# Early row maxima of a second attention layer: a fourth unit of queries, groups dealt out evenly, values ahead of the last score

## The chip, the cores and the metric

The kernel runs on one core of one Trainium2 chip. The metric is device time in microseconds (us) of one execution of the whole program, lower is better. Three runs of the kernel before the change took 2326.10, 2326.68 and 2327.10 us; the median is 2326.68 us. Engines are called by the profile's names: PE is the matmul engine (PEld is its weight load), DVE the vector engine, ACT the scalar engine, POOL the GpSimd engine, SP the queue that issues most DMAs.

## The reference

Two identical layers, with the same weights, on x of 2048 rows by 448: attention with 16 query heads of 28 that share one key head and one value head, then a gated linear unit.

```python
def _A_ref(x, wq, wk, wv, wo):              # H = 16, Dh = 28, S = 2048, D = 448
    q = (x @ wq).reshape(B, S, H, Dh).transpose(0, 2, 1, 3)
    k, v = x @ wk, x @ wv
    scores = jnp.einsum("bhqd,bkd->bhqk", q, k) * (Dh ** -0.5)
    o = jnp.einsum("bhqk,bkd->bhqd", softmax(scores), v)
    return o.transpose(0, 2, 1, 3).reshape(B, S, H * Dh) @ wo
def _B_ref(x, w_gate, w_up, w_down):        # F = 1792
    return (sigmoid(x @ w_gate) * (x @ w_up)) @ w_down

for _ in range(2):
    x = x + _A_ref(_layernorm(x), wq, wk, wv, wo)
    x = x + _B_ref(_layernorm(x), w_gate, w_up, w_down)
```

## The kernel before

**Tiles and steps.** A layer has 16 units of 128 queries (`u`) and 16 tiles of 128 keys (`kt`). The attention of a layer is a loop of 256 steps, one for each pair (u, kt), unit after unit. A step makes four score tiles of 128 keys by 512 (four heads by 128 queries) in PSUM (`s`, L591), ACT takes the exponential of each into a tile `P` (L594), and PE multiplies the four `P` of the step before with the values into one accumulator (`pv`, L602). The scores go into the exponential with the row maximum taken off already: the maximum of a query is one more row of the stationary operand `QS`.

**Row maxima.** So the maxima of a unit must be there before its first score. `Maxima` finds them with a pass of its own: the 2048 keys fall into ranges and the 16 heads into four sets, which gives 16 groups for each unit (for unit 0 of the second layer the last 512 keys are cut finer). A group is four matmuls side by side into four PSUM tiles `mx` (L556) and four DVE reductions `mp` (L561). After a unit's last group `row_max` closes it: two DVE operations, and a step later (`late`, `LT`) a transpose `mt` on PE, a copy `mr` on DVE and a DMA issued by POOL that puts the maxima into `QS` (L585). Groups of the first layer run one a step (`M` in `ORDER`), some unit ahead of the scores.

**PSUM.** One accumulator bank belongs to `pv`. All other PSUM tiles (`s`, `mx`, `qp`, `dn`, `wo`, `mt` and so on) share seven banks. A group of maxima takes four of them at once, and the next scores take what comes free.

**Other work of PE.** Between the pieces of a step, `fill.slice` (the `F` of `ORDER`) puts in matmuls of the rest of the layer: query projections `qp`, the gated unit (`gp`, `up`, `dn`) of blocks of 256 rows, and the output projection `wo` of a finished unit. A planner spreads what there is over the steps (`rate`). In the first 49 steps of the second layer there is little: eight query projections. The first block of the gated unit can start only when two units of attention are done and have passed through `Block.tile`, a list of stages that `tick` runs, each a given number of steps after the one before. Stage `fd` is the normalisation `xn` (L340) of such a unit on DVE; it reads a row factor `rs`, which six small POOL operations (L317 to L322) make.

**The seam between the layers.** The first layer ends with a loop that is no step of attention (L1088): it finishes the last gated blocks (`dn`, 42 matmuls for each 128 rows), and each 128 rows that are done give the next layer's keys: sum `x` (L801), statistics and `xn` on DVE, split `hl`, transposes `t`, key projection `kv`, `ktl`, transposes `kvt`. The second layer's first score needs the maxima of unit 0 over all keys, so it waits for the very last rows. While it waits, the loop takes early groups of the second layer: those of units 0, 1 and 2 (`AHEAD`) whose keys end at 1536 or before (`soon`), one in every two turns. The loop ends when all of them are done (`started`). What is left of units 1 and 2, and the first groups of later units, is done in the second layer's first 48 steps: in every even step, and in steps 5 and 11.

**Order.** Every engine works its instructions in the order in which the Python code issues them. The two lines that set it here:

```python
ORDER = "FSFSFSFSPXM"                                      # L1016
n = step % 2 == 0 or step in (5, 11)                       # L1051, second layer
```

Of the kernel before, what the change touches and what calls it, by code (L numbers as in the profile page):

```python
# [8 lines left out]
F32 = mybir.dt.float32  # L9
F16 = mybir.dt.float16  # L10
# [9 lines left out]
def interleaved_layers_kernel(ctx: ExitStack, tc: tile.TileContext, x, wq, wk, wv, wo, wg, wu, wd, out, layers=2):  # L20
# [6 lines left out]
    nc = tc.nc  # L27
# [3 lines left out]
    NT, NB, G, KT, FC = S // 128, S // 512, H // 4, S // 128, F // 128  # L31
    U = NT
# [429 lines left out]
    def load_qh(l, u):  # L462
        b, t = divmod(u, 4)
        if l + b == 0:
            QH[l, u] = QH0[:, :, t * 128:(t + 1) * 128]
            return
        assert QDONE[l, b] == G
        q = wk1.tile([128, G, 128], F16, name="QH", bufs=3)
        QH[l, u] = q
        nc.sync.dma_start(q, qd[l % 2][b, :, 0, :, t * 128:(t + 1) * 128].rearrange("g p n -> p g n"))  # L470

# [15 lines left out]
            out += [(kb, ka, kz, list(range(g, g + n))) for g in range(0, G, n)]  # L487
        return out

    AHEAD = (1, 2)  # L490

    def soon(u, kz):

        return (u == 0 or u in AHEAD) and kz <= S - 512

    class Maxima:
# [28 lines left out]

        def started(self):

            return not any(a[0] == 0 or soon(a[0], self.need(a)) for a in self.todo)

        def visit(self):  # L530
            for i in range(len(late) - 1, -1, -1):
# [4 lines left out]
        def step(self, a=None):  # L536
# [8 lines left out]
            todo = groups_of(l, u)  # L545
            kb, ka, kz, gs = todo[j]
            if u not in self.mp:
                self.mp[u] = wk1.tile([128, 4, 4, NB + 2], F32, name="mp", bufs=4)
            mp, qh = self.mp[u], QH[l, u]
            assert KVD[l] * 128 >= kz  # L550
            n, w = len(gs), kz - ka
# [20 lines left out]
    def row_max(l, u, mp, n):  # L572

        m32 = wk1.tile([128, 16], F32, name="m32")
        m16 = wk1.tile([128, 16], F16, name="m16")
        nc.vector.tensor_reduce(m32, mp.rearrange("p g h k -> p (g h) k")[:, :, :n], axis=AX.X, op=OP.max)
        nc.vector.tensor_scalar(m16, m32, -(2.0 ** -15), None, op0=OP.mult)

        def fin():
            stored.add(("m", l, u))  # L580
            p = fps([16, 128], F16, "mt")
            nc.tensor.transpose(p, m16, id16)
            r = wk1.tile([16, 128], F16, name="mr")
            nc.vector.tensor_copy(r, p)
            nc.gpsimd.dma_start(QS[l, u][28:29].rearrange("o g h n -> o (g h) n"), r)  # L585
        late.append([LT, fin, (l, u)])

    def scores(l, u, kt, g, P):
        assert ("m", l, u) in stored, (l, u, kt)
# [39 lines left out]
    class Block:  # L629
# [8 lines left out]
        def tile(self, u):  # L638
# [90 lines left out]
                return  # L729
                yield  # L730
            slow = 2 if l == 0 and u < 4 else 1
            return (1, f0), (1, fx), (slow, fy), (1, fz), (1, fw), (slow, fa), (slow, fb), (2, fc), (3, fd), (3, fe), (2, ff)

        def load_w(self, f):
            need(2 + f)
# [279 lines left out]
    early[0] = False  # L1015
    ORDER = "FSFSFSFSPXM"  # L1016
    MORE = (5, 10)
    HEAD = (U * KT - 32, U * KT - 28, U * KT - 16)
    FIRST = KT * TB + 17
    KEEP = 28000  # L1020
    VS = 1800
    for l in range(layers):
# [3 lines left out]
            late.pop(0)[1]()  # L1026
        if not l:
            mx.step()
        if not final:
            layer_tiles(l + 1)  # L1030
        if l:
# [5 lines left out]
        rate = 0.0  # L1037
        for step in range(U * KT):
            u, kt = divmod(step, KT)
            if step in HEAD and not final:  # L1040
                if step == HEAD[0]:
                    mxs[l + 1] = Maxima(l + 1)
                else:
                    load_qh(l + 1, HEAD.index(step))
            P = []
            for o in ORDER:
                if o == "S":
                    scores(l, u, kt, len(P), P)
                elif o == "M":
                    if l and step < KT * (1 + len(AHEAD)):  # L1050
                        n = step % 2 == 0 or step in (5, 11)  # L1051
                    else:
                        n = 1 + (u == 0 and kt in MORE)
                    if not n:
# [33 lines left out]
        while side or pend or (fill.gens if final else not nx.started()):  # L1088
# [5 lines left out]
            if a:  # L1094
                kz = nx.need(a)
                if soon(a[0], kz):
                    go = n >= 2
                elif kz == S - 128:
                    go = len(fine) > 1
                else:  # L1100
                    go = True
                if go:
                    nx.step(a)
                    n = 0
# [25 lines left out]
```

## Time and profile before

| quantity | value |
|---|---|
| median of three runs | 2326.68 us |
| the profiled execution, whole | 2324.3 us |
| its span, first to last instruction | 2321.3 us |
| mean granted clock of PE over the span | 0.987 |
| PE busy | 2225.1 us, 96% |
| DVE busy | 1638.1 us, 71% |
| ACT busy | 1585.8 us, 68% |
| POOL busy | 339.4 us, 15% |
| first score of the second layer | 1249.71 us from the span's start |
| first 48 steps of the second layer | 1250.1 to 1394.4 us |

How to read it: a busy share of 96% is an average over parts that differ. PE's spans are modelled and overlap the ones behind them, so a short wait of PE shows as a gap only where it is longer than that overlap; the distance from the start of one matmul to the start of the next shows it better. The idle time in square brackets of a timeline row is the engine's idle time just before that row, with the instruction that ended it.

### The profile page before, as it was taken

To read this page: it belongs to the slowest core of one execution; us is meant where nothing else is said; L and a number is where in the kernel's file an instruction comes from. 1 tells how busy PE (TensorE), PEld (TensorE's weight loads), DVE (VectorE), ACT (ScalarE), POOL (GpSimd) and SP (SyncE) were. 2 spreads that over 40 slices of the span, in tenths; PEclk is the share of its full clock that TensorE was granted. 3 is DMA by queue.
4 is the path that set the end of the run, shared out by engine and by line. 5 is a ranking of instruction groups with operands and counts; after the bars stand their busy time and mean duration, and the time that the engine had idled before them with its cause. 6 is when DMAs were issued, how large, how long until landed. Compare 5 with 4: busy or idle time off the path is not lost.

```text
span 2321.3 us, 41368 instructions
## 1 busy us (share of the span) xinstructions
PE 2225.1 (96%) x15786; PEld 1004.9 (43%) x15786; DVE 1638.1 (71%) x2908; ACT 1585.8 (68%) x2614; POOL 339.4 (15%) x606
## 2 busy tenths in 40 slices
PE   5898899999999999999999999999999999999999
PEld 3222244444444444444563224444444444444456
DVE  6888887777777777777884557767677777767322
ACT  6698777677767777776515887767676767767731
POOL 6204762100110110101002010000000000000010
PEclk9799999999999999999999999999999999999999
DMA  4244671423313132332341113223231313223233
GB/s 118 68 118 126 203 223 41 107 76 95 101 61 108 44 110 73 95 98 76 106 132 40 30 54 100 78 83 98 72 87 57 107 47 105 68 83 95 76 101 114
DMA packets 205639, 213.28 MB, mean 92 GB/s; under 512 B 137520, under 2 KB 165872, under 8 KB 205440
## 3 DMA queue, kind: packets, MB, share of 16 engines
q1 hardware_dynamic: 200064, 195.77, 28.9%
q0 software_dynamic: 5376, 14.87, 1.9%
q8 instruction: 123, 2.02, 0.4%
q14 instruction: 76, 0.62, 0.1%
HBM read 175.37 MB, written 23.59 MB: 86 GB/s over the span
## 4 chain that ended last, share of the span: by engine, by line
PE 57%; DVE 3%; DMA 1%; ACT 1%; issue 1%; SPq 0%; POOL 0%; DVEq 0%; POOLq 0%; ACTq 0%
PE pv L602 13%; PE s L591 12%; PE dn L791 8%; PE up L363 8%; PE gp L363 8%; PE mx L556 4%; DVE mp L561 2%; PE wo L702 2%; PE qp L363 1%; ACT P L594 1%; DMA wgu<-wgu_d 1%; SPq L459 0%; DVE oT L683 0%; DVE th L761 0%; DMA XT<-hl 0%
## 5 line engine op out<-in xcount | busy, mean ns | idle before, releaser
L594 ACT ACTIVATE P<-s,esc 128x512 f32<-128x512 f32 x2048 | 1323.8, 689 | 460.4 <-PE s L591 434.0
L561 DVE TENSOR_REDUCE mp<-mx 128x1 f32<-128x512 f32 x2048 | 1269.8, 683 | 422.0 <-PE mx L556 419.7
L591 PE MATMUL s<-QS,KK 96*128 96x512 f16 x2048 | 767.6, 383 | 42.4 <-DVE mp L561 20.8
L363 PEld LDWEIGHTS <-wgu 128*128 128x128 f16 x4928 | 457.9, 97 | 239.0 <-issue 95.9
L602 PE MATMUL pv<-P,VV 128*32 128x512 f32 x4096 | 548.8, 608 | 0.0
L363 PE MATMUL gp<-XT,wgu 128*128 128x256 f16 x2464 | 375.0, 273 | 0.0
L363 PE MATMUL up<-XT,wgu 128*128 128x256 f16 x2464 | 373.9, 273 | 0.5 <-ACT P L594 0.4
L791 PE MATMUL dn<-WD,h 128*128 128x448 f16 x1344 | 321.0, 353 | 0.0
L591 PEld LDWEIGHTS <-KK 96*128 96x128 f16 x2048 | 197.5, 97 | 155.6 <-issue 60.4
L556 PE MATMUL mx<-KK,QH 32*128 32x512 f16 (+1 forms) x2080 | 222.3, 386 | 10.0 <-ACT P L594 4.0
L556 PEld LDWEIGHTS <-QH 32*128 32x128 f16 x2080 | 53.9, 91 | 393.1 <-issue 390.6
L791 PEld LDWEIGHTS <-h 128*128 128x128 f16 x1344 | 124.1, 98 | 137.7 <-issue 25.5
L602 PEld LDWEIGHTS pv<-P,VV 128*32 128x32 f32 x4096 | 81.1, 108 | 200.4 <-issue 198.0
L764 ACT ACTIVATE h<-th 128x512 f16<-128x512 f32 x112 | 70.3, 628 | 108.5 <-DVE th L761 108.3
L676 POOL TENSOR_TENSOR lb<-pvs,lb 128x512 f32<-128x512 f32 x32 | 40.9, 1278 | 608.3 <-DMA lb<-sums 517.1
L317 POOL TENSOR_SCALAR rs<-mv 128x1 f32<-128x1 f32 (+2 forms) x52 | 12.2, 234 | 797.1 <-DVE mv L302 757.1
L363 PE MATMUL qp<-XT,WQ 128*128 128x512 f16 x352 | 117.7, 400 | 1.9 <-DVE mp L561 0.7
L765 DVE SCALAR_TENSOR_TENSOR h<-th,h 128x512 f16<-128x512 f32 x112 | 78.9, 704 | 34.5 <-ACT h L764 34.5
L753 ACT ACTIVATE th<-gp,gsc 128x512 f32<-128x512 f32 x112 | 76.6, 684 | 38.5 <-PE gp L363 38.4
L761 DVE SCALAR_TENSOR_TENSOR th<-th,up 128x512 f32<-128x512 f32 x112 | 76.1, 680 | 37.3 <-PE up L363 30.9
L702 PE MATMUL wo<-WO,oT 128*128 128x448 f16 x384 | 94.7, 358 | 4.4 <-ACT oT L682 4.3
L363 PEld LDWEIGHTS <-WQ 128*128 128x128 f16 x352 | 34.1, 100 | 67.2 <-issue 43.5
(134 smaller groups left out, 847.2 us busy)
## 6 DMA issues: line engine op xcount, KB each, us to landing
wgu<-wgu_d SPq DMA_DIRECT2D x224, 512.0 KB
QS<-qd SPq DMA_DIRECT2D x384, 32.0 KB
lb<-sums SPq DMA_DIRECT2D x128, 64.0 KB
xr<-in_A_x_dram SPq DMA_DIRECT2D x32, 224.0 KB
qd<-qst POOLq DMA_DIRECT2D x28, 256.0 KB, 2.6
wgu_d<-sgu POOLq DMA_DIRECT2D x14, 512.0 KB, 3.8
QH<-qd SPq DMA_DIRECT2D x28, 128.0 KB
x2d<-x SPq DMA_DIRECT2D x16, 224.0 KB
```

Source lines behind the costliest of these rows:

```text
L363: nc.tensor.matmul(ps, a, b, start=n == 0, stop=n == 10)
L556: nc.tensor.matmul(ps[h][:, i * w:(i + 1) * w], qh[32 * h:32 * h + 32, g], KK[l][32 * h:32 * h + 32, 1, ka:kz], start=True, stop=True, til ...
L561: nc.vector.tensor_reduce(o, ps[h].rearrange("p (g k) -> p g k", g=n), axis=AX.X, op=OP.max)
L591: nc.tensor.matmul(s, KK[l][0:96, 0, kt * 128:(kt + 1) * 128], QS[l, u][:, g].rearrange("p h n -> p (h n)"), start=True, stop=True)
L594: nc.scalar.activation(p, s, AF.Exp, scale=esc)
L602: nc.tensor.matmul(v[32 * g:32 * g + 32], VV[l][:, kt], P[g], start=kt == 0, stop=kt == KT - 1, tile_position=(0, 32 * g))
L702: nc.tensor.matmul(p, v["oT"][:, a, h * 128:(h + 1) * 128], WO[:, c, h], start=n == 0, stop=n == 11)
L753: defer(lambda: nc.scalar.activation(th, gp.rearrange("p j n -> p (j n)"), AF.Tanh, scale=gsc))
L761: nc.vector.scalar_tensor_tensor(t, th, 1.0, up.rearrange("p j n -> p (j n)"), op0=OP.add, op1=OP.mult)
L764: nc.scalar.activation(h[:, 0], t, AF.Copy, scale=2.0 ** -17)
L765: defer(lambda: nc.vector.scalar_tensor_tensor(h[:, 1], t, 2.0 ** -17, h[:, 0], op0=OP.mult, op1=OP.subtract), 1)
L791: nc.tensor.matmul(p, hs[f // 2][:, a, o:o + 128], WD[:, f, c], start=n == 0, stop=n == 3 * FC - 1)
```

## The change

Five edits, all for the second layer's first units:

- `AHEAD` takes in unit 3, and `started` asks only for unit 0's groups: the seam no longer has to finish the early groups. In the seam they are taken as long as `fine` is empty, that is, until the last 128 rows' `dn` is done.
- What is left of units 0 to 3, and two groups more, is dealt out evenly over the first 47 steps (`sparse`); here 21 groups where 26 stood in 48 steps.
- In a step behind one with a group, `LATER` sets the order: the values of the step before stand ahead of the fourth score, not behind it.
- The stage `fd` of the second layer's units 0, 1 and 2 comes one step later (4 steps behind the stage ahead of it, not 3).
- The maxima of units 1 to 3 are closed two visits after their last reduction, not one. The high halves of the first 512 queries are loaded at once into one tile `QHB` and the pool `QH` has two buffers, not three; `mp` has five, not four.

```diff
@@ -465,7 +465,14 @@
             QH[l, u] = QH0[:, :, t * 128:(t + 1) * 128]
             return
         assert QDONE[l, b] == G
-        q = wk1.tile([128, G, 128], F16, name="QH", bufs=3)
+        if b == 0:
+            if t == 0:
+                q = big.tile([128, G, 512], F16, tag="big", name="QHB")
+                nc.sync.dma_start(q, qd[l % 2][b, :, 0].rearrange("g p n -> p g n"))
+                for i in range(4):
+                    QH[l, i] = q[:, :, i * 128:(i + 1) * 128]
+            return
+        q = wk1.tile([128, G, 128], F16, name="QH", bufs=2)
         QH[l, u] = q
         nc.sync.dma_start(q, qd[l % 2][b, :, 0, :, t * 128:(t + 1) * 128].rearrange("g p n -> p g n"))
 
@@ -487,7 +494,7 @@
             out += [(kb, ka, kz, list(range(g, g + n))) for g in range(0, G, n)]
         return out
 
-    AHEAD = (1, 2)
+    AHEAD = (1, 2, 3)
 
     def soon(u, kz):
 
@@ -525,7 +532,7 @@
 
         def started(self):
 
-            return not any(a[0] == 0 or soon(a[0], self.need(a)) for a in self.todo)
+            return not any(a[0] == 0 for a in self.todo)
 
         def visit(self):
             for i in range(len(late) - 1, -1, -1):
@@ -545,7 +552,7 @@
             todo = groups_of(l, u)
             kb, ka, kz, gs = todo[j]
             if u not in self.mp:
-                self.mp[u] = wk1.tile([128, 4, 4, NB + 2], F32, name="mp", bufs=4)
+                self.mp[u] = wk1.tile([128, 4, 4, NB + 2], F32, name="mp", bufs=5)
             mp, qh = self.mp[u], QH[l, u]
             assert KVD[l] * 128 >= kz
             n, w = len(gs), kz - ka
@@ -583,7 +590,7 @@
             r = wk1.tile([16, 128], F16, name="mr")
             nc.vector.tensor_copy(r, p)
             nc.gpsimd.dma_start(QS[l, u][28:29].rearrange("o g h n -> o (g h) n"), r)
-        late.append([LT, fin, (l, u)])
+        late.append([2 if l and u in AHEAD else LT, fin, (l, u)])
 
     def scores(l, u, kt, g, P):
         assert ("m", l, u) in stored, (l, u, kt)
@@ -729,7 +736,7 @@
                 return
                 yield
             slow = 2 if l == 0 and u < 4 else 1
-            return (1, f0), (1, fx), (slow, fy), (1, fz), (1, fw), (slow, fa), (slow, fb), (2, fc), (3, fd), (3, fe), (2, ff)
+            return (1, f0), (1, fx), (slow, fy), (1, fz), (1, fw), (slow, fa), (slow, fb), (2, fc), (3 + (l and u < 3), fd), (3, fe), (2, ff)
 
         def load_w(self, f):
             need(2 + f)
@@ -1015,7 +1022,9 @@
     early[0] = False
     ORDER = "FSFSFSFSPXM"
     MORE = (5, 10)
-    HEAD = (U * KT - 32, U * KT - 28, U * KT - 16)
+    HEAD = U * KT - 32
+    sparse = ()
+    LATER = "FSFSFSPFSXM"
     FIRST = KT * TB + 17
     KEEP = 28000
     VS = 1800
@@ -1026,6 +1035,10 @@
             late.pop(0)[1]()
         if not l:
             mx.step()
+        else:
+            mx.todo.sort()
+            n = sum(a[0] < 4 for a in mx.todo) + 2
+            sparse = [i * (3 * KT - 1) // n for i in range(n)]
         if not final:
             layer_tiles(l + 1)
         if l:
@@ -1037,18 +1050,15 @@
         rate = 0.0
         for step in range(U * KT):
             u, kt = divmod(step, KT)
-            if step in HEAD and not final:
-                if step == HEAD[0]:
-                    mxs[l + 1] = Maxima(l + 1)
-                else:
-                    load_qh(l + 1, HEAD.index(step))
+            if step == HEAD and not final:
+                mxs[l + 1] = Maxima(l + 1)
             P = []
-            for o in ORDER:
+            for o in LATER if l and step < 3 * KT and step - 1 in sparse else ORDER:
                 if o == "S":
                     scores(l, u, kt, len(P), P)
                 elif o == "M":
-                    if l and step < KT * (1 + len(AHEAD)):
-                        n = step % 2 == 0 or step in (5, 11)
+                    if l and step < 3 * KT:
+                        n = step in sparse
                     else:
                         n = 1 + (u == 0 and kt in MORE)
                     if not n:
@@ -1094,7 +1104,7 @@
             if a:
                 kz = nx.need(a)
                 if soon(a[0], kz):
-                    go = n >= 2
+                    go = n >= 2 and not fine
                 elif kz == S - 128:
                     go = len(fine) > 1
                 else:
```

**DVE at the end of the seam.** `x` is the sum behind `dn` of the last rows but one (first) and of the last rows (second); `mp<-mx` are the reductions of groups, four for each; `ktl` belongs to the keys of the last rows but one. Before:

```order
L302 BN_AGGR mv<-st 128x2
L340 TENSOR_SCALAR xn<-x_15770,mv,rs 128x448
L333 TENSOR_TENSOR hl<-xn,hl 128x64
L334 TENSOR_TENSOR hl<-xn,hl 128x384
L394 SCALAR_TENSOR_TENSOR ktl_111<-kv,ktl_111 128x28
L396 COPY ktl_111<-ktl_111 128x6x28
L801 SCALAR_TENSOR_TENSOR x_15858<-dn,dsc,x_13913 128x448
```

And now:

```order
L302 BN_AGGR mv<-st 128x2
L568 TENSOR_REDUCE mp<-mx 128x1 x4
L340 TENSOR_SCALAR xn<-x_15791,mv,rs 128x448
L333 TENSOR_TENSOR hl<-xn,hl 128x64
L334 TENSOR_TENSOR hl<-xn,hl 128x384
L568 TENSOR_REDUCE mp<-mx 128x1 x8
L394 SCALAR_TENSOR_TENSOR ktl_111<-kv,ktl_111 128x28
L396 COPY ktl_111<-ktl_111 128x6x28
L808 SCALAR_TENSOR_TENSOR x_15915<-dn,dsc,x_13909 128x448
```

Three of the five groups that moved into the seam stand here: one ahead of `xn`, two ahead of the last rows' sum (the other two stand ahead of the first sum). On PE these two stand 18 `dn` and then 17 `dn`, seven transposes after the group ahead of them; the key projection and three `dn` follow the last one.

**DVE at steps 42 to 46 of the second layer**, from the statistics of unit 1's rows on. Before:

```order
L302 BN_AGGR mv<-st 128x2
L584 COPY mr<-mt 16x128
L340 TENSOR_SCALAR xn<-x_16612,mv,rs 128x448
L332 CAST hl<-xn 128x448
L561 TENSOR_REDUCE mp<-mx 128x1 x8
```

And now:

```order
L302 BN_AGGR mv<-st 128x2
L591 COPY mr<-mt 16x128
L568 TENSOR_REDUCE mp<-mx 128x1 x8
L340 TENSOR_SCALAR xn<-x_16626,mv,rs 128x448
L332 CAST hl<-xn 128x448
```

`xn` has moved behind the reductions of the group of step 44. (For unit 0, at steps 28 and 29, `xn` is one step later too, but the group of step 28 is gone, so that the next reductions still stand behind it.)

**PE from the last matmul of a group to the end of the next scores**, in steps 18 and 19 of before:

```order
L556 MATMUL mx<-KK,QH 128x512
L591 LDWEIGHTS KK
L591 MATMUL s<-QS,KK 128x512
L363 LDWEIGHTS WQ
L363 MATMUL qp<-XT_11716,WQ 128x512
L591 LDWEIGHTS KK
L591 MATMUL s<-QS,KK 128x512
L591 LDWEIGHTS KK
L591 MATMUL s<-QS,KK 128x512
L591 LDWEIGHTS KK
L591 MATMUL s<-QS,KK 128x512
L602 MATMUL pv<-P,VV 32x512 x4
```

And now in steps 11 and 12, the like place:

```order
L563 MATMUL mx<-KK,QHB 128x512
L598 LDWEIGHTS KK
L598 MATMUL s<-QS,KK 128x512
L598 LDWEIGHTS KK
L598 MATMUL s<-QS,KK 128x512
L363 LDWEIGHTS WQ
L363 MATMUL qp<-XT_11716,WQ 128x512
L598 LDWEIGHTS KK
L598 MATMUL s<-QS,KK 128x512
L609 MATMUL pv<-P,VV 32x512 x4
L598 LDWEIGHTS KK
L598 MATMUL s<-QS,KK 128x512
```

Four scores stood ahead of the values; now three do, and the fourth follows them.

## The prediction

> **What bounds the kernel now.** I read the page's busy shares first, then a table of stretches for the part that the change touches and for an equally long one behind it, then PE's waits there, and last the timelines of single stalls.
>
> ```profile
> PE 2225.1 (96%) x15786; PEld 1004.9 (43%) x15786; DVE 1638.1 (71%) x2908; ACT 1585.8 (68%) x2614; POOL 339.4 (15%) x606
> ...
> 1250.10:1394.40 144.30, 135.30 (x774) 35.37 (x772) 76.86 (x134) 122.01 (x204) 14.57 (x28) 0.96 0.13 36
> 1394.40:1538.70 144.30, 143.43 (x1037) 65.00 (x1036) 105.02 (x180) 104.10 (x166) 10.28 (x22) 1.00 0.29 86
> ```
>
> Over the whole span PE is the bound, and no edit takes PE work away. A gain must therefore come from PE's idle time or from its clock. In the second layer's first 48 steps (upper row of the table; its columns are PE, PEld, DVE, ACT, POOL busy, then PE's granted clock) PE is idle for 9.0 us and its clock is 0.96; in the next stretch it is idle for 0.9 us at clock 1.00. So the early steps are the place. ACT is busy for 122.0 of 144.3 us there and stands close behind PE; in the next stretch it is busy for 104.1. Who ends PE's waits there:
>
> ```profile
> PE s L591 <- DVE mp L561: 6.8, 16, 1.7
> PE s L591 <- DMA QS<-mr: 2.9, 1, 2.9
> PE s L591 <- ACT P L594: 0.8, 4, 0.2
> ...
> PE mt L582 <- DVE m L577: 0.3, 1, 0.3
> ...
> L594 ACT ACTIVATE P<-s,esc 128x512 f32<-128x512 f32 x193 | 118.7, 691 | 27.1 <-PE s L591 26.0
> ```
>
> Scores wait for reductions of maxima to free a PSUM bank (16 times, 6.8 us). The 2.9 us belong to the first score, at the end of the seam. The last row is ACT's group of exponentials in the same stretch: 118.7 / 193 = 0.61 us each.
>
> **The stage that moves a step.** Two of the 16 waits are large. The first, in step 29 (PE, POOL and DVE rows):
>
> ```profile
> 1334.52 0.40 PE L556 MATMUL mx<-KK,QH 32*128 32x512 f16 x4
> ...
> 1337.34 0.59 PE L591 MATMUL s<-QS,KK 96*128 96x512 f16 x2 [1.45 <-DVE mp L561]
> ...
> 1335.52 0.19 POOL L322 TENSOR_TENSOR rs<-rs 128x1 f32<-128x1 f32 x1
> ...
> 1335.75 0.51 DVE L340 TENSOR_SCALAR xn<-x,mv,rs 128x448 f32<-128x448 f32 x1 [2.10 <-POOL rs L322]
> 1336.29 0.40 DVE L332 CAST hl<-xn 128x448 f16<-128x448 f32 x1
> 1336.60 2.48 DVE L561 TENSOR_REDUCE mp<-mx 128x1 f32<-128x512 f32 x4
> ```
>
> The group's matmuls start at 1334.52, but its reductions stand behind `xn`, which waits for POOL until 1335.75. They start at 1336.60, and the scores wait 1.45 us. A step later `rs` is long there. At unit 0 no group of step 28 is left to be held up; at unit 1 the reductions of step 44 stand ahead of `xn`. The second such wait costs more:
>
> ```profile
> 1384.36 1.01 PE L591 MATMUL s<-QS,KK 96*128 96x512 f16 x2 [1.68 <-DVE mp L561]
> 1385.30 1.94 PE L602 MATMUL pv<-P,VV 128*32 128x512 f32 x8
> ...
> 1384.10:1387.50 3.40, 3.14 (x11) 0.44 (x11) 2.01 (x4) 1.26 (x2) 0.96 (x2) 0.50 0.35 69
> ```
>
> It is 1.68 us long, and the granted clock is 0.50 for the 3.4 us behind it: another 1.7 us. Together 1.45 + 1.68 + 1.7 = 4.8 us. An ordinary wait behind a group stays (0.4 us each, below), so I take **-4.0 us**; bounds -2.0 (the clock falls all the same and 0.6 us stay each time) and -4.8.
>
> A rule of the Trainium skill speaks against a part of this: "TensorE: Matmul & The Clock Gate", section "What's actually happening", lets the clock fall to half only after an idle window of some 3.4 us, and calls the window free-running. The trace differs: the clock fell at a wait of 1.68 us, and did not at one of 1.45 us. By the rule the low clock would have another cause and stay; the term would be -2.3 us instead of -4.0 us and the time 2323.3 us, which lies in the forecast's own case below.
>
> **Five groups leave the 48 steps.** 26 groups become 21. What a group costs PE, and what PE waits behind it, at three places (steps 18, 26 and 36):
>
> ```profile
> 1303.79 1.07 PE L602 MATMUL pv<-P,VV 128*32 128x512 f32 x8
> 1304.79 0.40 PE L556 MATMUL mx<-KK,QH 32*128 32x512 f16 x4
> 1305.12 0.39 PE L591 MATMUL s<-QS,KK 96*128 96x512 f16 x1
> ...
> 1305.57 0.77 PE L591 MATMUL s<-QS,KK 96*128 96x512 f16 x2
> 1306.56 0.38 PE L591 MATMUL s<-QS,KK 96*128 96x512 f16 x1 [0.22 <-DVE mp L561]
> ...
> 1305.21 2.48 DVE L561 TENSOR_REDUCE mp<-mx 128x1 f32<-128x512 f32 x4 [3.04 <-PE mx L556]
> ...
> 1329.60 0.39 PE L591 MATMUL s<-QS,KK 96*128 96x512 f16 x1
> 1330.43 0.38 PE L591 MATMUL s<-QS,KK 96*128 96x512 f16 x1 [0.45 <-DVE mp L561]
> 1331.03 0.59 PE L591 MATMUL s<-QS,KK 96*128 96x512 f16 x2 [0.22 <-DVE mp L561]
> ...
> 1357.84 0.60 PE L591 MATMUL s<-QS,KK 96*128 96x512 f16 x2
> ```
>
> By starts a group takes 0.33 us of PE (1304.79 to 1305.12), a score 0.22 (the last row: two in 0.60, of which 0.38 is one's own length), the values 1.0 us (1303.79 to 1304.79). Behind the first group the scores at 1305.57 and 1306.56 are 0.99 us apart where two scores take 0.44: 0.55 us lost. Behind the second, 1329.60 to 1331.03 is 1.43 us for two scores: 0.99 lost. Behind the third nothing is lost. The mean is 0.5; I take 0.4, because the 14 small listed waits sum to only 3.7 us (6.8 less 1.45 and 1.68). Five groups: 5 x 0.33 + 5 x 0.4 = **-3.65 us** in this stretch; bounds -1.65 and -6.6 (0.99 each).
>
> **Values ahead of the fourth score.** In the first place above, the third score waits for the first reduction and the fourth for the second. With 1.0 us of values between them the second wait goes (0.38 us by starts: the third score begins at 1305.57 + 0.77 - 0.38 = 1305.96, the fourth 0.60 us later where 0.22 would do). The first wait stays, since three scores still follow the group. And the group's tiles fall on other banks now: by the built program's addresses the first bank goes to the second or third score nearly as before, and a wait for the second bank ahead of the values is left behind four of the 20 groups; I count eight before. So four waits of 0.38 go: **-1.5 us**. What it can cost: the fourth exponential starts 1.0 us later. ACT's room is (144.3 - 122.0) / 48 = 0.46 us a step now. Bounds: -4.0 us (ten waits go) and +4.0 us (0.2 us for each of 20 groups, PE waiting for ACT). The transposes `mt`, a visit later, lose a wait of 0.3 us: **-0.3**.
>
> **What the seam pays.** The five groups are done there: 5 x 0.33 = 1.65 us of PE ahead of the last `dn`, at a place without idle time. That is not all, because the last rows' chain hangs behind them (PE and DVE rows):
>
> ```profile
> 1228.50 0.55 PE L346 MATMUL t<-id,hl 128*128 128x128 f16 x7
> 1228.89 1.49 PE L791 MATMUL dn<-WD,h 128*128 128x448 f16 x7
> 1230.21 0.45 PE L363 MATMUL kv<-WKV,XT 128*128 128x56 f16 x11
> 1230.50 0.73 PE L791 MATMUL dn<-WD,h 128*128 128x448 f16 x3
> ...
> 1232.90 3.62 PE L363 MATMUL qp<-XT,WQ 128*128 128x512 f16 x16
> 1236.36 0.66 PE L346 MATMUL t<-id,hl 128*128 128x128 f16 x7
> ...
> 1249.71 0.61 PE L591 MATMUL s<-QS,KK 96*128 96x512 f16 x2 [2.90 <-DMA QS<-mr]
> ...
> 1231.11 0.20 DVE L396 COPY ktl<-ktl 128x168 f16<-128x168 f16 x1
> 1231.27 0.68 DVE L801 SCALAR_TENSOR_TENSOR x<-dn,dsc,x 128x448 f32<-128x448 f32 x1
> ...
> 1236.07 0.55 DVE L334 TENSOR_TENSOR hl<-xn,hl 128x384 f16<-128x384 f32 x1
> ```
>
> The last group comes between the second and the third of these PE rows. In the time of before plus what the groups ahead of it add (four, 1.3 us) it starts at about 1231.5. Its four reductions take 2.48 us from 0.4 us later, then `ktl` takes 0.3: the sum `x` starts at about 1234.7, where 1231.27 + 1.65 = 1232.9 would do. So DVE adds 1.8 us, and the chain from `x` to the first score is moved by 3.4 to 3.6 us. Is there slack in it? `hl` ends at 1236.62, and its transposes start at 1236.36, at once behind 16 `qp`: none. What is late next is these transposes; PE waits about 1.5 us for them. I take **+3.6 us**; bounds +1.65 (the order hides it) and +5.3 (that wait makes the clock fall as the one of 1.68 us did, 1.7 us).
>
> **Step 50.** Unit 1's stages end a step later, so the first gated block feeds step 51, not 50, and step 50 has no filler:
>
> ```profile
> 1396.53 0.39 PE L556 MATMUL mx<-KK,QH 32*128 32x512 f16 x4
> ...
> 1399.70 0.39 PE L556 MATMUL mx<-KK,QH 32*128 32x512 f16 x4
> ```
>
> Step 49, with four `qp`, is 3.17 us from group to group. Without filler PE has 4 x 0.22 + 1.0 + 0.33 = 2.2 us of work, and the DVE reductions of 2.48 us and the bank waits decide. What PE loses there, some 0.8 of the 3.17 us, does not come back, because all later steps are full: **+0.8 us**; bounds 0 and +1.6. The one larger load of `QHB`, the smaller pool and `mp` cost nothing: the load is issued at step 224 of the first layer and first read 13 steps later.
>
> **The sum.** -4.0 - 3.65 - 1.5 - 0.3 + 3.6 + 0.8 = -5.05 us. It is made against the profiled execution: span 2321.3 us, whole 2324.3 us, which gives 2319.25. The median of the runs is 2.4 us above that execution, so the forecast is 2326.68 - 5.05 = **2321.6 us**. The ends: with all terms at their best -14.05, at their worst +6.95.
>
> **Rivals.**
>
> *The seam hides the groups.* If the delayed sum is taken up by the 2.9 us that the first score waits for the DMA of `QS`, the seam pays only 1.65 us: -7.0 us, 2319.7 us. For it: POOL issues that DMA behind stores of `qp` results, so the maxima have slack there. Against it: those `qp` stand behind the same transposes on PE and move along.
>
> *The seam eats it.* The wait at the last transposes drops the clock (+1.7 us), and the groups lose only their 0.33 us: -5.05 + 1.7 + 2.0 = -1.4 us, 2325.3 us. The row at 1384.10 is for it. The clock rule of the Trainium skill cited above is against it, since it lets no wait of 1.5 us change the clock.
>
> *ACT becomes the bound (the slower end).* In a stretch shorter by 9.45 us, ACT's room is (144.3 - 9.45 - 122.0) / 48 = 0.27 us a step. A fourth exponential that starts 1.0 us late has two steps' room, 0.54 us; if ACT can't work ahead, each of 20 groups costs 0.46 us, 9.2 us in all, in place of the gain of 1.5: -5.05 + 1.5 + 9.2 = +5.65, 2332.3 us. Slower by over 0.2% begins at 0.41 us a group. Against it: `P` has eight buffers, and scores come 0.22 us apart where ACT needs 0.61, so that work for ACT queues up quickly.
>
> *It does not do what it says.* Twelve groups of unit 3 should come early. By the built order only five more run in the seam: eight of unit 3 take the place of later ones. That is in the sum already.
>
> **How the numbers follow.** The forecast (-2.9 to -7): 0.52; the groups hidden in the seam or more waits gone (below -7): 0.18; the seam eats it (-2.9 to +2): 0.23; ACT the bound: 0.07. A change of 0.2%, 4.65 us, is about what a measurement of this kernel can tell from none. Of the forecast's own case a little over two thirds lies beyond that line (0.36), the rest on this side (0.16). So faster 0.36 + 0.18 = 0.54, the same 0.16 + 0.23 = 0.39, slower 0.07. The range leaves out the very best and the slower case: 2316.5 to 2327.0 us.
>
> **What would show it.** Right: no wait of over 1 us at steps 29 and 45 and no half clock there; PE's idle time in the first 48 steps down by about half and the stretch some 9 us shorter; the sum of the last rows on DVE directly behind eight reductions and `ktl`, and the first score about 3.6 us later. Wrong: the first score moved by under 2 us, or ACT without idle time in the early steps while scores wait for `P`.

## The result, and the profile after

| quantity | before | after |
|---|---|---|
| median of 12 runs each, us | 2326.39 (2320.30 to 2330.56) | 2321.74 (2318.48 to 2323.18) |
| ratio, 95% interval | | 0.9977 [0.9969, 0.9985] |
| span of the profiled execution, us | 2321.3 | 2316.7 |
| mean granted clock of PE | 0.987 | 0.986 |

The change takes 4.65 us off, 0.2%; the interval lies below 1 but reaches across the line of 0.2%. The totals of the page hardly differ:

```profile
PE 2223.1 (96%) x15786; PEld 1004.4 (43%) x15786; DVE 1639.0 (71%) x2908; ACT 1585.4 (68%) x2614; POOL 339.0 (15%) x606
```

So the two traces are compared by pieces, each cut at the same instruction in both. *Seam*: from the first of the last 84 `dn` of the first layer (two times 128 rows) to the first score of the second layer. *Steps 0-1, 2-47, 48-83*: from the first exponential of the first step to the first exponential behind the last.

| piece, us | before | after | difference |
|---|---|---|---|
| up to the seam | 1214.50 | 1215.33 | +0.83 |
| seam | 35.21 | 39.19 | +3.98 |
| to the first exponential | 0.43 | 0.64 | +0.21 |
| steps 0-1 | 7.05 | 6.59 | -0.46 |
| steps 2-47 | 137.20 | 127.26 | -9.94 |
| steps 48-83 | 144.13 | 144.40 | +0.27 |
| the rest | 782.76 | 783.29 | +0.53 |

The first row is no result of the change: in all kernels below it lies between 1211.95 and 1221.00 us, and it scatters alike whatever was edited. That is why small effects are read from the pieces and not from spans of single executions.

**The early steps of after.** The table of stretches (PE, PEld, DVE, ACT, POOL busy, then PE's clock) for steps 0 to 47 and an equally long stretch behind, and who ends PE's waits in the first of them (us in total, times, longest):

```profile
1255.10:1389.00 133.90, 129.09 (x754) 34.94 (x752) 64.50 (x114) 121.27 (x203) 14.97 (x28) 0.98 0.14 39
1389.00:1522.90 133.90, 132.65 (x954) 59.93 (x953) 98.25 (x168) 97.02 (x154) 9.94 (x21) 1.00 0.27 81
...
PE s L598 <- DVE mp L568: 2.2, 7, 0.6
PE s L598 <- ACT P L601: 1.5, 5, 0.7
```

PE's idle time has gone from 9.0 to 4.8 us, the waits for reductions from 6.8 us (16 times) to 2.2 us (7 times), and none is longer than 0.6 us. The clock has risen from 0.96 to 0.98: the half clock near 1384 us is gone, the one at the first score is left. ACT's room is (133.90 - 121.27) / 48 = 0.26 us a step, and scores wait for it 1.5 us in all.

**The seam of after.** The timeline of PE:

```profile
1231.06 0.55 PE L346 MATMUL t<-id,hl 128*128 128x128 f16 x7
1231.45 1.49 PE L798 MATMUL dn<-WD,h 128*128 128x448 f16 x7
1232.88 0.40 PE L563 MATMUL mx<-KK,QHB 32*128 32x512 f16 x4
...
1236.24 3.62 PE L363 MATMUL qp<-XT,WQ 128*128 128x512 f16 x16
1240.76 0.49 PE L346 MATMUL t<-id,hl 128*128 128x128 f16 x4 [0.91 <-ACT hl L332]
1241.49 0.34 PE L346 MATMUL t<-id,hl 128*128 128x128 f16 x3 [0.24 <-DVE hl L334]
...
1254.52 1.89 PE L598 MATMUL s<-QS,KK 96*128 96x512 f16 x4 [2.89 <-DMA QS<-mr]
```

The timelines of DVE and POOL at the same place:

```profile
1229.94 2.48 DVE L568 TENSOR_REDUCE mp<-mx 128x1 f32<-128x512 f32 x4
1233.30 2.48 DVE L568 TENSOR_REDUCE mp<-mx 128x1 f32<-128x512 f32 x4 [0.88 <-PE mx L563]
1235.70 0.18 DVE L394 SCALAR_TENSOR_TENSOR ktl<-kv,ktl 128x28 f16<-128x28 f32 x1
1235.79 0.19 DVE L396 COPY ktl<-ktl 128x168 f16<-128x168 f16 x1
1235.90 0.68 DVE L808 SCALAR_TENSOR_TENSOR x<-dn,dsc,x 128x448 f32<-128x448 f32 x1
...
1249.61 0.21 DVE L591 COPY mr<-mt 16x128 f16<-16x128 f16 x1 [0.32 <-PE mt L589]
...
1251.68 0.72 POOL L435 DMA_DIRECT2D qd<-qst  x1 [0.30 <-POOL qst L428]
1252.40 0.53 POOL L592 DMA_DIRECT2D QS<-mr  x1
```

The first rows are DVE's, the last two POOL's. The sum `x` of the last rows stands directly behind the last group's reductions and `ktl`. It starts 20.57 us behind the seam's first `dn`, 3.80 us later than before. PE then waits 0.91 + 0.24 us at the last transposes. From `x` to the first score it is 18.62 us, against 18.44 before, and the first score still waits 2.89 us for the DMA of `QS`. That DMA is not waiting for the maxima: `mr` is ready at 1249.82, and POOL issues the DMA at 1252.40, behind two stores of `qp` results.

**The moved stage in after.** DVE at unit 0 (first two rows) and at unit 1 (last two):

```profile
1336.64 0.51 DVE L340 TENSOR_SCALAR xn<-x,mv,rs 128x448 f32<-128x448 f32 x1 [2.10 <-POOL rs L322]
...
1338.11 2.48 DVE L568 TENSOR_REDUCE mp<-mx 128x1 f32<-128x512 f32 x4 [0.53 <-PE mx L563]
...
1379.92 2.48 DVE L568 TENSOR_REDUCE mp<-mx 128x1 f32<-128x512 f32 x4 [2.17 <-PE mx L563]
1382.33 0.50 DVE L340 TENSOR_SCALAR xn<-x,mv,rs 128x448 f32<-128x448 f32 x1
```

At unit 0 `xn` still waits 2.10 us for `rs`, but no reductions are ready behind it: the next ones wait for PE. At unit 1 it stands behind a group's reductions and no longer waits.

### The profile page after: what moved, and what is told of

Its sections match the earlier page's. It is cut to its first block, busy times and chain, and to the rows that moved or that the text cites. A ratio compares the mean times of both kernels' runs of the same rounds, so it can differ in the third digit from the quotient of the medians.

```text
span 2316.7 us, 41363 instructions
## 1 busy us (share of the span) xinstructions
PE 2223.1 (96%) x15786; PEld 1004.4 (43%) x15786; DVE 1639.0 (71%) x2908; ACT 1585.4 (68%) x2614; POOL 339.0 (15%) x606
## 4 chain that ended last, share of the span: by engine, by line
PE 58%; DVE 3%; ACT 1%; DMA 1%; issue 1%; POOL 0%; SPq 0%; DVEq 0%; ACTq 0%; POOLq 0%
PE pv L609 13%; PE s L598 12%; PE dn L798 8%; PE up L363 8%; PE gp L363 8%; PE mx L563 4%; PE wo L709 2%; DVE mp L568 2%; ACT P L601 1%; PE qp L363 1%; DMA wgu<-wgu_d 0%; DVE th L768 0%; DVE oT L690 0%; DMA rc<-sums 0%; DVE st L301 0%
## 5 line engine op out<-in xcount | busy, mean ns | idle before, releaser
L563 PE MATMUL mx<-KK,QH 32*128 32x512 f16 x1792 | 195.0, 391 | 8.2 <-ACT P L601 3.5
L563 PEld LDWEIGHTS <-QH 32*128 32x128 f16 x1792 | 46.8, 91 | 354.4 <-issue 352.5
```

Of the source, the lines that this page charges most:

```text
L563: nc.tensor.matmul(ps[h][:, i * w:(i + 1) * w], qh[32 * h:32 * h + 32, g], KK[l][32 * h:32 * h + 32, 1, ka:kz], start=True, stop=True, til ...
```

## The experiments

Pieces of every kernel, in us, from its own trace, the last column its longest wait of a score in steps 2 to 47. Where the text below gives no interval, the kernel ran once:

| kernel | seam | steps 0-1 | steps 2-47 | steps 48-83 | longest wait |
|---|---|---|---|---|---|
| before | 35.21 | 7.05 | 137.20 | 144.13 | 1.68 |
| after | 39.19 | 6.59 | 127.26 | 144.40 | 0.7 |
| e1: after, stage `fd` back | 39.18 | 7.06 | 127.30 | 144.13 | 0.7 |
| e2: after, old order everywhere | 39.17 | 6.34 | 128.55 | 144.40 | 0.6 |
| e3: before + stage `fd` later | 35.21 | 7.06 | 133.10 | 144.41 | 0.5 |
| e4: after, one group less in the seam | 36.92 | 7.05 | 127.30 | 144.41 | 0.2 |
| e5: after, five less in the seam | 35.20 | 7.67 | 128.57 | 144.41 | 0.7 |
| e6: after, groups in steps 0, 2, 4, ... | 39.18 | 6.56 | 127.51 | 144.40 | 0.4 |
| e7: before + values ahead of the last score | 35.21 | 6.79 | 136.11 | 144.05 | 1.60 |
| e9: even dealing, later closing, smaller edits | 35.21 | 7.60 | 128.90 | 144.13 | 0.6 |
| e12: even dealing, smaller edits | 35.21 | 6.67 | 129.94 | 144.14 | 0.6 |
| e11: before + `fd` later, no neighbours | 35.22 | 7.05 | 134.67 | 152.89 | 0.5 |
| e8: e4 + e1 + maxima of unit 0 by SP | 34.49 | 4.67 | 127.26 | 144.13 | 0.2 |
| e10: e8 with e5 in place of e4 | 33.16 | 6.54 | 129.47 | 144.14 | 0.7 |

Steps 0-1 are to be read with care: in all kernels but e8 they lie at least in part in the half clock behind the first score, and where that begins differs from one execution to the next. After and e1 have the same program there, and took 6.59 and 7.06 us. Steps 2-47 repeat far better (127.26, 127.30, 127.30 and 127.26 us in after, e1, e4 and e8), but in some executions the half clock still reaches into step 2, in before by 0.64 us.

**e1: the stage at its old step.**

```diff
-return (1, f0), ..., (2, fc), (3 + (l and u < 3), fd), (3, fe), (2, ff)
+return (1, f0), ..., (2, fc), (3, fd), (3, fe), (2, ff)
```

> The changed kernel with the normalisation stage fd back at 3 steps for all units. Measured by the profile: the early stretch (first exponential of step 0 to that of step 48 of the second layer) was 144.25 us before the change and is 133.86 us after it. My theory (the reductions of a group wait behind xn, which waits for POOL): at unit 0 nothing comes back, because the group of step 28 is gone and the next reductions are a step later; at unit 1 the group of step 44 stands behind xn again, with its wait of about 1.7 us and the half clock behind it. Early stretch 133.9 + 3.0 = 136.9 us; step 50 has filler again, so the stretch from step 48 to 84 is 0.3 us shorter (144.1). Rival (the even spacing alone keeps reductions and xn apart): early stretch 133.9 us, no wait over 1 us. Second rival (both waits come back): 138 us or more.

Measured: 2319.92 us, 0.9962 [0.9948, 0.9976]; steps 2-47 take 127.30 us, as after, with no half clock near step 45 and 0.27 us less in steps 48-83. My theory, that the large waits come back, fell. The timelines of DVE and POOL at step 43 of this kernel show why:

```profile
1379.37 1.86 DVE L568 TENSOR_REDUCE mp<-mx 128x1 f32<-128x512 f32 x3
1381.16 0.49 DVE L340 TENSOR_SCALAR xn<-x,mv,rs 128x448 f32<-128x448 f32 x1
...
1383.40 2.48 DVE L568 TENSOR_REDUCE mp<-mx 128x1 f32<-128x512 f32 x4 [1.29 <-PE mx L563]
...
1380.61 0.19 POOL L322 TENSOR_TENSOR rs<-rs 128x1 f32<-128x1 f32 x1
```

With the new dealing a group's reductions stand between the statistics and `xn`, so POOL's `rs` (ready at 1380.80) is there when DVE comes to `xn` at 1381.16; the next group comes later. At unit 0 `xn` waits 2.10 us for `rs`, as it does in after, and no reductions are ready behind it. The new dealing removes the same waits as the moved stage does.

**e2: the old order everywhere.**

```diff
-for o in LATER if l and step < 3 * KT and step - 1 in sparse else ORDER:
+for o in ORDER:
```

> The changed kernel with the values behind the fourth score in every step, as before. My theory: four waits of 0.38 us for the second bank come back, early stretch 133.9 + 1.5 = 135.4 us. Rival one (the order of values and fourth score is most of the gain, since it takes the wait behind nearly every one of 20 groups): 133.9 + 6 = 140 us. Rival two (it costs as much in late exponentials as it saves): 133.9 us within 0.5, or less. The seam does not move in any of them (39.2 us from the first dn of the last 256 rows to the first score).

Measured: 2323.12 us, 0.9984 [0.9975, 0.9993]. Steps 2-47 are 1.29 us longer, and scores wait for reductions 3.4 us (15 times) where it was 2.2 us (7 times):

```profile
PE s L598 <- DVE mp L568: 3.4, 15, 0.5
```

**e3: before, with the stage a step later and nothing else.**

```diff
-return (1, f0), ..., (2, fc), (3, fd), (3, fe), (2, ff)
+return (1, f0), ..., (2, fc), (3 + (l and u < 3), fd), (3, fe), (2, ff)
```

> The kernel before with one edit: fd of the second layer's first three units a step later. My theory: both large waits (1.45 and 1.68 us) and the half clock go, less the ordinary wait that stays: early stretch 144.25 - 4.0 = 140.2 us; the stretch from step 48 to 84 gets 0.3 us longer; seam as before (35.2 us). Rival (the low clock was not caused by the wait of 1.68 us): half clock somewhere near step 45 all the same, early stretch 142 us.

Measured: 2323.07 us, 0.9983 [0.9973, 0.9992]. Steps 0 to 47 are 4.09 us shorter (144.25 to 140.16), the half clock near step 45 is gone with the wait, steps 48-83 are 0.28 us longer. Alone the moved stage is worth what was expected of it; beside the even dealing (e1) it is worth nothing. What is left in this kernel:

```profile
PE s L591 <- DVE mp L561: 4.5, 17, 0.5
```

**e4 and e5: fewer groups in the seam.** They run in the early steps in place of it (22 and 26 there, dealt out evenly). An early group is then taken there only until the last gated block has its rows, or while more than a given amount of filler is left; e5 has 25000 where e4 has 12000:

```diff
-go = n >= 2 and not fine
+go = n >= 2 and not fine and (BLK[l, NBL - 1].fed < TB or fill.left > 12000)
```

> The changed kernel without the last of the five groups in the seam, the one whose reductions stand directly ahead of the last rows' sum; it is dealt into the early steps (22 groups there). My theory (that sum waits for four reductions): the seam is 39.2 us now and gets 1.8 us (DVE) and 0.33 us (PE) shorter, 37.1 us; the early stretch gets 0.4 to 0.7 us longer, 134.4 us; net -1.5 us. Rival (the seam's end is set by POOL's queue, not by the chain from the sum): the seam gets 0.33 us shorter, 38.9 us, net 0.

> The changed kernel with none of the five groups in the seam behind the start of the last 256 rows' dn; 26 groups are dealt evenly into the early steps. The stretch from step 2 to step 48 is used, since steps 0 and 1 lie in the half clock behind the seam: 137.20 us before the change, 127.26 us after it. My theory (a group costs PE 0.33 us and a wait of 0.4 us): 127.26 + 3.65 = 130.9 us, seam 35.2 us as before the change. Rival (the early steps are bound by ACT, and with the groups well spaced one more costs next to nothing, as the 0.04 us of one group more in run e4_seam_one_less suggests): 127.3 to 128 us; then moving groups into the seam was a loss of up to 4 us, paid for by the spacing.

Measured, e4: 2319.82 us, 0.9966 [0.9953, 0.9979]. The sum `x` comes 2.07 us earlier and the seam is 2.27 us shorter, while one more group costs steps 2-47 only 0.04 us. DVE in e4, where the sum `x` is no longer held up by reductions; it stands behind `ktl`, which waits for ACT:

```profile
1235.61 2.48 DVE L568 TENSOR_REDUCE mp<-mx 128x1 f32<-128x512 f32 x4
1239.24 0.19 DVE L394 SCALAR_TENSOR_TENSOR ktl<-kv,ktl 128x28 f16<-128x28 f32 x1 [1.16 <-ACT VV L393]
1239.35 0.19 DVE L396 COPY ktl<-ktl 128x168 f16<-128x168 f16 x1
1239.50 0.68 DVE L808 SCALAR_TENSOR_TENSOR x<-dn,dsc,x 128x448 f32<-128x448 f32 x1
```

e5, one run: 2318.7 us. The seam is that of before. Of the five groups four stand in steps 2-47 and cost 1.31 us together; the fifth stands in step 1, in the half clock behind the first score. It costs 1.08 us there against after, and 0.61 us against e1, whose steps 0-1 have the same program as after's. 1.31 / 4 = 0.33 us is just a group's time on PE: on balance the four bring no new wait. The list has fewer waits for reductions than in after:

```profile
PE s L598 <- DVE mp L568: 1.0, 3, 0.4
```

So five groups in the seam cost 3.99 us and bring 1.31 + 0.61 = 1.92 us, or 2.39 us by after's steps 0-1.

**e6: every second step in place of the even dealing.**

```diff
-sparse = [i * (3 * KT - 1) // n for i in range(n)]
+sparse = [2 * i for i in range(n)]
```

> The changed kernel with its 21 groups in the even steps 0 to 40, not dealt over 47. My theory (their number counts, not their places, as long as xn does not hold them up): steps 2 to 48 in 127.3 us, plus or minus 0.7. Rival (the even spacing is the gain): 129 us or more, with waits for the reductions of over 1 us or more of the small ones.

Measured, one run: 2319.74 us; steps 2-47 take 127.51 us, 0.25 more than after. With 21 groups their exact steps hardly count.

**e7: before, with the values ahead of the last score.**

```diff
-for o in ORDER:
+for o in LATER if l and step < 3 * KT and step and (step % 2 or step in (6, 12)) else ORDER:
```

> The kernel before with one edit: in a step behind one with a group, values ahead of the fourth score. My theory: waits for the second bank go, 1.3 to 3 us of them; steps 2 to 48 in 137.20 - 2 = 135.2 us, and the two large waits behind xn stay, shorter by up to the 1.0 us of the values (if the scores that wait are the last ones) or not at all (if they stand ahead of the values). Rival (no gain alone): 137.2 us.

Measured, one run: 2325.08 us; steps 2-47 are 1.09 us shorter. Both large waits stay (1.14 and 1.60 us), and the half clock of 3.4 us behind the second:

```profile
PE s L591 <- DVE mp L561: 4.3, 7, 1.6
```

Seven waits in place of 16: the order takes the small ones away (6.8 - 4.3 = 2.5 us in the list) and gives part of it back in waits for `P`, as the list has 1.6 us for scores and 1.4 for groups where before had 0.8 and 0.6.

**e9 and e12: the dealing without stage, order and seam.** e9 is after with the edits of e1, e2 and e5, so that the 26 groups, the order and the stage are as before, and the dealing and the closing of the maxima are new. The smaller edits of the change stay in too: groups of unit 3 in place of later ones, `QHB`, and five buffers for `mp`. e12 takes the closing back:

```diff
-late.append([2 if l and u in AHEAD else LT, fin, (l, u)])
+late.append([LT, fin, (l, u)])
```

> The changed kernel without LATER, with fd at 3 steps and with none of the five groups in the seam: what stays is that 26 groups are dealt evenly over 47 steps (and closed a visit later), with unit 3's early groups in the place of later ones. Steps 2 to 48 were 137.20 us before the change, 133.10 with fd alone moved (e3_before_fd), 128.57 with fd, LATER and even dealing (e5_seam_five_less). Theory A (even dealing is the largest part, and makes the moved fd needless): 128.57 + 1.3 = 129.9 us, no wait over 1 us. Theory B (fd is needed where 26 groups stand): 132 to 134 us, with one or two waits over 1 us. Theory C (even dealing does nothing): 136 us or more. Seam 35.2 us in all.

> The run with the 26 groups dealt out evenly, none of the five in the seam, and the old order and stage step, but with the maxima of units 1 to 3 closed one visit after their last reduction, as before the change. It asks whether it is the even dealing or the later closing that makes steps 2 to 48 of that run 128.90 us, where the kernel before with the moved stage alone needs 133.10 us. Theory A (the dealing): PE gets back only the waits at the transposes of the maxima, 0.3 us once to three times; 129.2 to 129.9 us, waits for reductions stay near the 1.3 us of that run. Theory B (the closing): the transposes take the bank and the place on DVE that the scores then wait for; 132 us or more, waits for reductions near the 4.5 us of the kernel with the moved stage. If it comes between, 130 to 132 us, both carry a part.

Measured, one run each: e9 2320.58 us, e12 2313.72 us (its first layer happens to be the shortest of all: 1211.95 us up to the seam). Steps 2-47 take 129.94 us in e12 and 128.90 us in e9. PE's waits in e9, and behind them those in e12:

```profile
PE s L598 <- ACT P L601: 1.8, 5, 0.6
PE s L598 <- DVE mp L568: 1.3, 6, 0.2
```

```profile
PE s L598 <- DVE mp L568: 2.1, 10, 0.2
PE s L598 <- ACT P L601: 1.4, 5, 0.6
```

The dealing, with those smaller edits, takes 137.20 - 129.94 = 7.26 us off, the closing a visit later 1.04 more. One group of the 25 that before had in these steps stands in step 1 now, 0.33 us of it.

**e11: before with the stage moved, and no groups in neighbouring steps.** Is the dealing's gain that steps 5 and 11 no longer have a group? Their two groups are put behind step 48:

```diff
-n = step % 2 == 0 or step in (5, 11)
+n = step % 2 == 0
-n = 1 + (u == 0 and kt in MORE)
+n = 1 + (u == (3 if l else 0) and kt in MORE)
```

> The kernel before with fd a step later (as e3_before_fd) and without the two groups in steps 5 and 11; they are done in steps 53 and 58, two groups each there. So no two groups follow each other in the first 48 steps. Theory A (two groups in neighbouring steps wait for each other's reductions, which even dealing avoids): steps 2 to 48 in 133.1 - 3 = 130 us or less. Theory B (a group more or less costs 0.26 us, as from 21 to 26 in the evenly dealt kernels, wherever it stands): 132.6 us; then the gain of even dealing has another source, such as the places of unit 1's to 3's groups against the other work.

Measured, one run: 2333.52 us. The run can't be read as it was meant to: the maxima of unit 3 come too late for step 48, whose first score waits 3.2 us for them.

```profile
PE s L591 <- DMA QS<-mr: 6.1, 2, 3.2
```

A half clock of 6.8 us follows, and steps 48-83 take 152.89 us. What can be read lies ahead of it: steps 4 to 13 take 27.38 us against 29.14 in e3, 0.88 us for each of the two groups that are gone. So a group between two others costs more than its 0.33 us. But the even dealing of 26 has neighbours as well (steps 0-1, 9-10, 18-19, 27-28, 36-37), and e3's other groups wait too; neighbours alone are not the reason.

**e8 and e10: what the runs pointed to.** e8 is after with the edits of e4 and e1, and SP, which has nothing in its way there, issues the DMA of unit 0's maxima. e10 is the same with e5's edit in place of e4's.

```diff
-nc.gpsimd.dma_start(QS[l, u][28:29].rearrange("o g h n -> o (g h) n"), r)
+(nc.sync if l and u == 0 else nc.gpsimd).dma_start(QS[l, u][28:29].rearrange("o g h n -> o (g h) n"), r)
```

> The changed kernel with three more edits: one group less in the seam (as in e4_seam_one_less), fd back at 3 steps (as in e1_undo_fd), and the DMA that puts unit 0's maxima of the second layer into QS issued by SP, not by POOL. That DMA stood in POOL's queue behind two stores of query projections, 2.6 us after its data were ready, and the first score waited 2.9 us for it; behind that wait PE ran at half clock for 6.8 us. My theory: seam 36.9 - 2.5 = 34.4 us; the wait becomes shorter than 0.6 us and the half clock behind it does not come, so that steps 0 and 1 take 5.2 us instead of 6.6 to 7.1 and step 2 some 0.4 us less; early stretch 132 us; from step 48 to 84 144.1 us. In all some 11 us below the kernel before (ratio 0.995). Rival (SP's DMA takes as long to land, or its queue is full): seam 36.9 us, ratio 0.9965 as e4_seam_one_less. Second rival (the half clock has another cause): seam 34.4 us, steps 0 and 1 as slow as now.

> e8_best with none of the five groups in the seam (26 in the early steps). From e8_best: seam 34.49 us, early stretch 131.93 us. Theory (the groups in the seam are a loss): seam 35.2 - 2.5 = 32.7 us; early stretch 131.9 + 1.3 = 133.2 us; the two together 0.5 us shorter than in e8_best; ratio about 0.9945. Rival (the seam is now bound by PE's or POOL's other work): seam 34 us or more, and the sum longer.

Measured, e8: 2313.56 us, 0.9947 [0.9934, 0.9961]: the interval lies wholly below that of after. In PE's timeline of e8 the first score waits 0.45 us in place of 2.89:

```profile
1249.50 1.04 PE L598 MATMUL s<-QS,KK 96*128 96x512 f16 x4 [0.45 <-DMA QS<-mr]
```

The seam is 2.43 us shorter than in e4, the half clock behind it is gone, and steps 0-1 take 4.67 us in place of 7.05. e10: 2313.55 us, 0.9942 [0.9928, 0.9956], the same within the intervals. Its profiled execution has a seam shorter by 1.33 us and steps 0 to 47 longer by 4.08 us, with a wait of 0.85 us and a half clock of 3.4 us; which of the two is better stays open.

## Why the prediction came out right, and what in it was not

The time was right (2321.6 forecast, 2321.74 measured), and each of its three pieces was within 1 us: the seam +3.98 (forecast +3.6), the early steps -10.40 (-9.45), steps 48-83 +0.27 (+0.8). The parts inside the early steps were not right: terms that were too large made up for one that was left out. So the closeness of the time is luck. It is also closer than a single execution can show: the 12 runs of after lie between 2318.48 and 2323.18 us.

- **What bounds the kernel:** right. The gain lies in the first 48 steps: PE's waits, its half clock and the groups that left.
- **The moved stage, -4.0 us:** right for the edit alone (e3: -4.09 us; the half clock went with its wait, as forecast), wrong for its place in the sum. Beside the even dealing it brings nothing (e1: 0.04 us), since that dealing parts `xn` from the late `rs` as well, and costs 0.27 us behind step 48. The step that failed is that I priced it on the order of before, though the order of groups around it changes too.
- **Five groups leave, -3.65 us:** mis-sized. Their PE time was right (0.33 us each), the wait of 0.4 us behind each wasn't. Its reason, 3.7 us of small waits, is 0.14 us for each of 26 groups; with even dealing, order and stage changed, none is added on balance (e5). They are worth 1.31 us in steps 2-47 and 0.61 to 1.08 in step 1, some 2 us in all.
- **The even dealing:** the prediction has no term for it; it only counted how many groups leave. It is the largest part: -7.26 us of steps 2-47 (e12, with the smaller edits), of which some 4 us are the two waits and the half clock that e3 also removes. Of the other 3.16 us, 0.33 is the group that went to step 1, and some 1.9 are small waits in the lists (those for reductions 4.5 us in 17 in e3, 2.1 us in 10 in e12, with 0.8 us more for `P`, and 0.3 less elsewhere). The lists don't show the rest. The later closing of the maxima, forecast -0.3, gives 1.04 (e9). Dealing with closing (-8.30), then order and stage (-0.33, e9 to e5), then the five groups (-1.31) make the -9.94 us.
- **Values ahead of the fourth score, -1.5 us:** right in size in the changed kernel (e2: 1.29) and in before (e7: 1.09), with waits for reductions at 7 in place of 15 or 16. The count was not right: with the old order eight waits of some 0.15 us come back (e2: 3.4 us in place of 2.2), not four of 0.38. Among 26 evenly dealt groups it and the stage together bring only 0.33. ACT was not hurt beyond 1.5 us of waits: the rival in which ACT becomes the bound fell.
- **The seam, +3.6 us:** right, and by its mechanism: `x` 3.80 us later, directly behind eight reductions and `ktl`, and PE waiting 1.15 us for the last transposes where some 1.5 was expected. The wait had no half clock behind it, so the rival of the seam that eats the gain fell as well. So did the one that it hides the groups: the wait of 2.9 us for `QS` stayed, since POOL's stores set that time and they moved along. e4 shows how thin the place is: the last group alone costs 2.27 us there.
- **Step 50, +0.8 us:** half right. Step 50 of after has no filler and takes 3.07 us (1394.33 to 1397.40) for the 2.2 us of work that the prediction counts, so the loss there is as priced. But steps 48-83 are longer by only 0.27 to 0.28 us (e1, e3): that none of it comes back was wrong. Where it comes back was not followed up.

So the change is faster mostly by what its dealing does; moving groups into the seam was a loss of 3.99 - 1.92 = 2.1 us (1.6 us by after's steps 0-1).

What stays open: why even dealing lowers the small waits beyond e3's. By e11's steps 4 to 13 the crowding around steps 5 and 11 may be 2 x (0.88 - 0.33) = 1.1 us of it, an estimate. Which PSUM bank each score gets was not tried apart from the steps of the groups, e11 failed as a test of the whole, and no run takes unit 3's groups, `QHB` or the fifth `mp` buffer out of e12.

## What to carry to other kernels

Before edits that remove the same waits are summed, ask of each what it does when the other is there; only one alone and one undone (e3 and e1) tell the two answers. Work that is moved to a place without idle time on PE is to be priced by the chain behind it, on every engine that it passes: a group of 0.33 us on PE cost 2.27 us where its reductions stood ahead of the last sum. A total that comes out right does not show that its terms were. A DMA that ends a wait should be issued by a queue with nothing ahead of it: in e8 that cut the first score's wait from 2.89 to 0.45 us.

## What the runs showed of the hardware

The drops of PE's granted clock lie on a grid in time. In each execution all stretches at half clock behind the first layer's start-up begin a whole multiple of 3.413 us apart and last whole multiples, but for one that the program's end cuts: in before at 1251.00 and 1384.12, 39 times 3.413 us; in e11 at 1253.37, 1393.31 and 1420.62, 41 and 8 times. In e7 they are 1251.55 and 1384.67. Where the grid lies differs from one execution to the next. The Trainium skill ("TensorE: Matmul & The Clock Gate", "What's actually happening") states a free-running window of that length, and the trace agrees.

The same section asks for an idle window ahead of half clock. The trace differs: PE needn't be idle for the whole window. Tables of stretches cut on the grid (length, then PE, PEld, DVE, ACT, POOL busy and the clock), of before: the grid cut the wait of 1.45 us in 0.44 and 1.01 us, and that of 1.68 us in 1.44 and 0.24, so that most of the second lies in one window:

```profile
1336.33:1339.75 3.42, 2.41 (x14) 0.56 (x13) 2.75 (x5) 1.95 (x4) 1.17 (x2) 1.00 0.17 34
1339.75:1343.16 3.41, 3.19 (x22) 0.90 (x25) 1.91 (x4) 3.41 (x7) 0.00 (x0) 1.00 0.18 34
1380.71:1384.12 3.41, 1.77 (x14) 0.33 (x7) 1.38 (x4) 2.70 (x5) 2.40 (x8) 1.00 0.00 0
1384.12:1387.53 3.41, 3.17 (x11) 0.44 (x11) 1.99 (x4) 1.26 (x2) 0.94 (x2) 0.50 0.35 69
```

The same of e11, and of the seam of e1:

```profile
1417.21:1420.62 3.41, 2.39 (x21) 0.73 (x14) 2.59 (x5) 0.28 (x1) 0.00 (x0) 1.00 0.45 98
1420.62:1424.03 3.41, 3.41 (x14) 1.92 (x14) 2.88 (x5) 1.87 (x3) 0.00 (x0) 0.50 0.64 259
```

```profile
1244.84:1248.25 3.41, 2.10 (x36) 0.91 (x35) 2.69 (x6) 1.23 (x4) 1.88 (x2) 1.00 0.51 148
1248.25:1251.66 3.41, 3.41 (x32) 1.58 (x33) 2.15 (x4) 1.46 (x3) 0.60 (x1) 1.00 0.06 20
```

PE was busy for 1.77 us of the window ahead of the half clock in before and for 2.39 us in e11; in the seam of e1, with 2.10 us, nothing followed, nor in that of e12 with 1.47 us (1242.78 to 1246.19). So busy time alone doesn't decide, and what else counts (the seam's matmuls are mostly of 128 by 128, those of the steps smaller) was not tried. What follows a wait also depends on where the grid happens to lie in an execution: the first score's wait of 2.9 us had 6.8 us of half clock behind it in eleven traces and 3.4 us in e12. Part of the scatter of single executions should come from there; how much was not measured.
